# Value loads of the late attention tiles: issued by SyncE instead of ScalarE

## The chip, the cores and the metric

The kernel runs on one core of a Trainium2 chip. The metric is the device time of one execution in microseconds (us). Five engines run their own instruction streams in program order: TensorE (PE, its weight loads PEld), VectorE (DVE), ScalarE (ACT), GpSimd (POOL) and SyncE (SP). SP only issues DMA transfers here; ACT and POOL issue some beside their computing. An engine that issues a DMA first waits for whatever the transfer depends on, and all that stands behind it on that engine waits with it.

## What is computed

A chunked attention with memory slots, and two gated feed-forward layers on its output. All inputs of the attention are float32.

```python
def _attn_ref(q, k, v, mem_k, mem_v):            # q, k, v: (4, 8, 768, 64); mem: (4, 8, 8, 64)
    chunk, left_ctx, right_ctx = (32, 16, 8)
    for c in range(S // chunk):
        q_c = q[:, :, c_start:c_end]
        k_full = concatenate([mem_k, k[:, :, l_start:r_end]], axis=2)
        v_full = concatenate([mem_v, v[:, :, l_start:r_end]], axis=2)
        a = softmax(scale * q_c @ k_full.T)
        out[:, :, c_start:c_end] = a @ v_full

x = attn_out.transpose(0, 2, 1, 3).reshape(3072, 512)
x = sigmoid(x @ w_gate) * (x @ w_val) @ w_out         # moe:  512 -> 1536 -> 512
h = x @ w_in;  out = (h * sigmoid(1.702 * h)) @ w_out # moe2: 512 -> 2048 -> 512
```

## The kernel before

The 3072 tokens are cut in two ways: into 32 attention tiles of 96 queries (three chunks each, eight per batch entry), and into six blocks of 512 columns for the matrix products. Blocks 0 to 3 go through the first feed-forward layer one after the other (`first_product` L821 and L828, `gated`, `gemm2` L1020); blocks 4 and 5, and then the whole second layer, use another scheme of products (L1318, L1655). Each float32 product is done as three passes over a high and a low part, so that PE has work in nearly all of the time.

Attention for blocks 1 to 5 is woven into those products. Nine tiles are done early by a path with PE transposes. The other 23, the **late tiles**, are walked in a fixed order, `nth` = 0 to 22. For one of them:

- SP loads the queries in 12 small transfers and the keys in some 16 to 20 for each pair of tiles (`f<-in_q_dram`, `raw<-in_k_dram`, and `f<-in_mem_k_dram` for each new batch entry). Both have two sets of buffers. DVE turns them (`ev_q` L532, `ev_k` L540), ACT adds the memory keys (`ev_m` L544).
- PE does one **burst**: first the products with the values (`pe_pv`, L704) of an older tile, then the scores of this tile (`pe_s`, L555). From the fourth tile on, the burst of tile n holds the values' products of tile n-2, from a list `late` of tiles not yet finished.
- The softmax follows on DVE, ACT and POOL; then `rest()` of the tile that came before: it loads that tile's values and memory values into `vn`, POOL scales its probabilities, and DVE turns them into `pt` (L670). `evict` takes the burst's result to the next layer's input (L758, L761), or, for blocks 4 and 5, through `qt` (L733) to a scratch tensor by a store that ACT issues (`x_dram<-qt`).

There is one buffer `vn` for all late tiles. The value load of tile n-1 has therefore to wait for the burst of tile n, whose products read the values of tile n-2, and has to land before the burst of tile n+1. A value load is one transfer of up to 120 rows and one of the 8 memory rows; a tile at the start or the end of a batch entry has a third one, for its clamped edge rows. Over the 23 late tiles that makes 28 + 23 = 51 transfers.

The order of all instructions on all engines is written by the class `Schedule`, a planner in the kernel file: tasks have an engine, an estimated length and dependencies; due times are passed back from the products and from the bursts (burst n is due at 150 + 12.6 n us by `PACE`, L388), and at each step the ready task with the earliest due time goes next on its engine. In `dma()` (L345) the issue of a transfer is a task of 0.45 us on "sp", or on "act" where `act=True`; key loads are given 0.62 us. The due time of a task on "sp" is passed back with 2.0 us and its bytes' time added for the landing (`lat`, L66), that of a task on "act" without. So the argument `act` changes the plan as well as the issuing engine.

ACT also issues the stores of the first layer's results (`y_dram<-f`, L1044). In the same stage SP loads, after the last queries, the inputs of the next stage (L1194, L1304, L292).

Of the kernel before, what the change touches and what calls it, by code (L numbers as in the profile page):

```python
# [136 lines left out]
def c_act(n):  # L137
    return 0.13 + n / 1200.0
# [7 lines left out]
def kernel(  # L146
# [198 lines left out]
    def dma(dst, src, key, r=(), act=False, dur=0.45, pool=False):  # L345
        n = 8
        for d in src.shape:
            n *= d
        q_ = nc.gpsimd if pool else nc.scalar if act else nc.sync
        add("pool" if pool else "act" if act else "sp", dur, lambda: q_.dma_start(out=dst(), in_=src), r=list(r), w=[key], nbytes=n)  # L350
# [39 lines left out]
    def attention(t, bufs, banks, pe_path, extra=None, nth=0, last=False):  # L390
# [11 lines left out]
        def tadd(eng, dur, fn, r=(), w=(), more=0.0, **kw):  # L402
            add(eng, dur, fn, r=r, w=w, slack=SL + more, **kw)

        def load_ctx(name, src, mem, act=False):

            s0 = j * TQ - LEFT
            r0 = LEFT if j == 0 else 0
            r1 = TK - RIGHT if j == TPB - 1 else TK
            parts = [(r0, r1, src[b, :, s0 + r0 : s0 + r1, :]), (TK, P, mem[b])]  # L410
            if j == 0:
                parts.append((0, LEFT, src[b, :, 0:LEFT, :]))
            if j == TPB - 1:
                parts.append((r1, TK, src[b, :, S - RIGHT : S, :]))
            ks = []
            for i, (a, z, s) in enumerate(parts):
                ks.append((kk[name], i))
                dma(lambda a=a, z=z: T[name][a:z], s.rearrange("h s d -> s h d"), ks[-1], r=pre, act=act)
            for i in range(len(parts), 4):
                ks.append((kk[name], i))  # L420
            return ks
# [197 lines left out]
        def norm(eng, dst, rows_, keys):  # L619
            r = slice(*rows_)  # L620
            c = slice(*keys)
            n = rows_[1] - rows_[0]
            eng.tensor_tensor(  # L623
                out=dst, in0=e3()[r, :, c], in1=T["sm"][r].to_broadcast([n, H, keys[1] - keys[0]]), op=ALU.mult
            )

        if pe_path:

            def ev_norm(c):
                r = (c * CH, (c + 1) * CH)  # L630
                eng = nc.vector if en[c] == "dve" else nc.gpsimd
                norm(eng, T["pw"][r[0] : r[1], :, c * CH : c * CH + CTX], r, (0, CTX))

            def ev_norm_m():
                norm(nc.vector if en[0] == "dve" else nc.gpsimd, T["pw"][:, :, TK:P], (0, TQ), (CTX, KW))

            en = ["pool", "pool", "pool"] if t in (0, 2) else ["dve", "pool", "pool"]
            for c in range(NCK):
                tadd(en[c], 0.75 if en[c] == "dve" else 1.2, lambda c=c: ev_norm(c), r=ke + [kk["sm"]], w=[(kk["pw"], c)])
            tadd(en[0], 0.25 if en[0] == "dve" else 0.35, ev_norm_m, r=ke + [kk["sm"]], w=[(kk["pw"], 3)])  # L640

            def pe_pt(n):
                for h in range(H):
                    a, p = divmod(h, NP)
                    nc.tensor.transpose(  # L645
                        bt[a][:, p * TQ : p * TQ + n], T["pw"][:n, h, :], ident()[:n, :n]
                    )

            def ev_pt(a, n):
                src = bt[a][:, : NP * TQ].rearrange("p (h s) -> p h s", s=TQ)[:, :, :n]  # L650
                dst = T["pt"].rearrange("p (a h) s -> p a h s", a=2)[:, a, :, :n]
                nc.scalar.activation(dst, src, AF.Copy)

            def probs(n, more=()):
                bands = range(4) if n == TQ else (0, 3)
                r = [(kk["pw"], c) for c in bands] + [bufs.kid, *more]
                tadd("pe", 0.7 if n == TQ else 0.45, lambda: pe_pt(n), r=r, w=kbt, margin=mg)
                for a in range(2):
                    tadd("act", c_act(NP * n), lambda a=a: ev_pt(a, n), r=[kbt[a]], w=[(kk["pt"], a)])
        else:  # L660

            def ev_norm():
                norm(nc.gpsimd, T["pn"][0:L, :, 3 * CH - NM : 3 * CH], (0, L), (CTX, KW))
                norm(nc.gpsimd, T["pn"][L:TQ, :, CTX:KW], (L, TQ), (CTX, KW))

            PTB = ((0, 0, 0), (1, 0, 1), (2, 0, 2), (0, 1, 1), (1, 1, 2), (2, 1, 3), (0, 2, 3), (1, 2, 3))

            def ev_pt(part):
                for c, kb, r in PTB[2 * part : 2 * part + 2]:
                    nc.vector.transpose(  # L670
                        T["pt"][r * CH : (r + 1) * CH, :, c * CH : (c + 1) * CH],
                        T["pn"][c * CH : (c + 1) * CH, :, kb * CH : (kb + 1) * CH],
                    )

            def rest():
                load_ctx("vn", v, mem_v, True)
                tadd(
                    "pool",
                    0.95,
                    lambda: norm(nc.gpsimd, T["pn"][:, :, 0:CTX], (0, TQ), (0, CTX)),  # L680
                    r=ke + [kk["sm"]],
                    w=[(kk["pn"], 0)],
                )
                tadd("pool", 0.6, ev_norm, r=ke + [kk["sm"]], w=[(kk["pn"], 1)])
                for part in range(4):
                    tadd(
                        "dve",
                        0.88,
                        lambda part=part: ev_pt(part),
                        r=[(kk["pn"], 0), (kk["pn"], 1)],  # L690
                        w=[(kk["pt"], part)],
                    )
# [74 lines left out]
        if pe_path and t != NPRO - 1:  # L767
            probs(TQ)
            tadd("pe", 0.8, pe_pv, r=rp, w=[kbv], margin=mg)
            evict()  # L770
        elif pe_path:
            probs(CH)
            tadd("pe", 0.5, lambda: pe_pv(CH), r=rp, w=[kbv])
            evict(0)
            probs(TQ, [kbv])
            tadd("pe", 0.8, lambda: pe_pv(TQ, bq), r=rp, w=[kbq])
            held_back.append(lambda: evict(1, bq, [kbq]))
        else:
            late.append(dict(pv=pe_pv, rp=rp, evict=evict, rest=rest))
            if last:  # L780
                for x in list(late):
                    if x is not late[0]:
                        x["rest"]()
                    tadd("pe", 0.9, x["pv"], r=x["rp"], w=[kb0, kb1])
                    x["evict"]()
                late.clear()
# [1113 lines left out]
```

## Time and profile before

| | |
|---|---|
| time, median of three | 1128.76 us (1127.51 to 1131.07) |
| the profiled execution's own time | 1130.38 us |
| its span | 1128.6 us |
| busy in the span: PE / DVE / ACT / POOL | 1116.4 / 842.4 / 589.6 / 161.6 us |
| share of PE in the chain that ended last | 97% |
| granted TensorE clock | 1.00 in all stages |
| DMA queue of SP (q1) | 201560 packets, 162.29 MB |
| DMA queue of ACT (q10) | 37368 packets, 15.47 MB |

The span counts from the first to the last instruction; 1.8 us of the execution's time lie around it. The late tiles run from about 133 us (first query load on SP) to 460 us. Matmuls are pipelined and their ends modelled, so a busy PE says only that no gap between them was seen.

### The profile page before, as it was taken

Reading aid. Unit: us, or ns where it says so; the run is one execution under the profiler, and the core shown is the slowest. Engines: PE = TensorE matmul, PEld = TensorE weight load, DVE = VectorE, ACT = ScalarE, POOL = GpSimd, SP = SyncE. Lnnn points to the kernel's source line nnn. Section 1 sums busy time; section 2 is a strip of 40 time slices with the busy share of each in tenths; the row PEclk is TensorE's granted clock in tenths of the full one; section 3 lists DMA queues with packets and bytes.
Section 4 is the critical chain, followed back from the end, with each engine's and each line's share of the span. In section 5 each row is a group of like instructions: output and inputs, shape, how many; then the busy total and the mean of one; then the engine's idle time right before and its main releaser. Section 6 shows DMA issues by size and latency. Waiting matters only on the chain.

```text
span 1128.6 us, 19515 instructions
## 1 busy us (share of the span) xinstructions
PE 1116.4 (99%) x7190; PEld 933.7 (83%) x7190; DVE 842.4 (75%) x1440; ACT 589.6 (52%) x972; POOL 161.6 (14%) x209
## 2 busy tenths in 40 slices
PE   7999999999999999999999999999999999999998
PEld 6888899997888888888888888888888888888886
DVE  7989746776767788888887788869966369575365
ACT  5888632222222344676666777666455365354452
POOL 4332244122333113200001110000000000000000
PEclk9999999999999999999999999999999999999999
DMA  9676344335433555542556867868796666776526
GB/s 208 203 216 196 90 122 114 52 67 119 102 83 79 150 145 174 199 161 104 177 178 245 305 216 269 271 244 295 245 255 211 200 203 219 233 216 204 170 86 176
DMA packets 245903, 203.13 MB, mean 180 GB/s; under 512 B 170928, under 2 KB 191920, under 8 KB 245808
## 3 DMA queue, kind: packets, MB, share of 16 engines
q1 hardware_dynamic: 201560, 162.29, 48.9%
q0 software_dynamic: 6880, 24.12, 5.7%
q10 hardware_dynamic: 37368, 15.47, 5.0%
q8 instruction: 57, 0.93, 0.3%
q14 instruction: 38, 0.31, 0.1%
HBM read 151.49 MB, written 50.33 MB: 179 GB/s over the span
## 4 chain that ended last, share of the span: by engine, by line
PE 97%; DMA 1%; SPq 1%; ACT 0%; DVE 0%; issue 0%; ACTq 0%
PE bank L1318 30%; PE bank L1655 20%; PE bank L1020 18%; PE bank L821 15%; PE bank L828 8%; PE both L704 2%; PE both L555 2%; SPq L350 1%; PE bank L704 1%; PE bank L885 0%; DMA kn<-in_mem_k_dram 0%; PE bank L645 0%; DMA vn<-in_v_dram 0%; DMA w<-wo_dram 0%; PE both L645 0%
## 5 line engine op out<-in xcount | busy, mean ns | idle before, releaser
L1318 PE MATMUL bank<-sb_x,sb_r 128*128 128x512 f32 x1512 | 347.4, 389 | 0.0
L1318 PEld LDWEIGHTS bank<-sb_x,sb_r 128*128 128x128 f32 x1512 | 283.8, 188 | 58.9
L1655 PE MATMUL bank<-wq,w 128*128 128x512 f32 x756 | 178.0, 389 | 0.4 <-DMA w<-wo_dram 0.4
L1655 PEld LDWEIGHTS bank<-wq,w 128*128 128x128 f32 x756 | 141.8, 188 | 30.3 <-issue 0.8
L821 PE MATMUL bank<-xh,w 128*128 128x512 f32 (+1 forms) x464 | 159.6, 355 | 0.0
L821 PE MATMUL bank<-xl,w 128*128 128x512 f32 (+1 forms) x464 | 158.6, 353 | 0.0
L1334 DVE TENSOR_TENSOR sb_s<-bank,sb_s 128x512 f32<-128x512 f32 x108 | 74.4, 690 | 83.0 <-PE bank L1318 75.8
L828 PE MATMUL bank<-xh,w 128*128 128x512 f32 (+1 forms) x464 | 108.8, 356 | 0.0
L1020 PE MATMUL bank<-gh,wq 128*128 128x512 f32 (+1 forms) x448 | 98.7, 360 | 0.0
L821 PEld LDWEIGHTS bank<-xh,w 128*128 128x128 f32 x464 | 87.8, 189 | 12.6
L821 PEld LDWEIGHTS bank<-xl,w 128*128 128x128 f32 x464 | 87.8, 189 | 11.9
L1330 ACT ACTIVATE sb_s<-bank 128x512 f32<-128x512 f32 x108 | 64.8, 604 | 50.7 <-PE bank L1318 49.9
L828 PEld LDWEIGHTS bank<-xh,w 128*128 128x128 f32 x464 | 78.1, 189 | 12.4
L1020 PEld LDWEIGHTS bank<-gh,wq 128*128 128x128 f32 x448 | 76.4, 189 | 12.9
L670 DVE STREAM_TRANSPOSE pt<-raw 32x256 f32<-32x256 f32 x184 | 79.5, 432 | 4.7 <-POOL raw L623 2.1
L1626 DVE TENSOR_TENSOR wq<-xh_g,wq 128x1024 fp32r<-128x1024 f32 (+1 forms) x60 | 60.5, 1008 | 22.9 <-ACT wq L1623 22.5
L1623 ACT ACTIVATE wq<-xh_g 128x1024 fp32r<-128x1024 f32 (+1 forms) x60 | 53.3, 889 | 35.2 <-PE bank L1655 34.2
L853 ACT ACTIVATE gh<-sig 128x512 fp32r<-128x512 f32 (+1 forms) x58 | 32.3, 557 | 67.4 <-DVE sig L848 61.6
L623 POOL TENSOR_TENSOR raw<-e,sm 96x448 f32<-96x448 f32 (+2 forms) x69 | 41.0, 606 | 176.1 <-DVE sm L615 149.0
L1655 PE MATMUL bank<-wq,w_e 128*128 128x512 f32 x252 | 62.5, 389 | 0.0
L845 ACT ACTIVATE sig<-bank 128x512 f32<-128x512 f32 (+1 forms) x58 | 30.5, 526 | 55.5 <-PE bank L828 49.7
L1655 PEld LDWEIGHTS bank<-wq,w_e 128*128 128x128 f32 x252 | 47.3, 188 | 9.8
(215 smaller groups left out, 1646.1 us busy)
## 6 DMA issues: line engine op xcount, KB each, us to landing
sb_r<-wc_dram SPq DMA_DIRECT2D x133, 256.0 KB
w<-wo_dram SPq DMA_DIRECT2D x63, 512.0 KB
w_e<-wo_dram SPq DMA_DIRECT2D x21, 512.0 KB
wc_dram<-sb_r SPq DMA_DIRECT2D x15, 512.0 KB
wo_dram<-w POOLq DMA_DIRECT2D x14, 512.0 KB, 3.9
raw<-in_moe_w_out_dram SPq DMA_DIRECT2D x13, 512.0 KB
raw<-in_moe_w_in_dram SPq DMA_DIRECT2D x13, 512.0 KB
wf_dram<-f POOLq DMA_DIRECT2D x24, 256.0 KB, 2.9
```

What stands on the lines that cost most here:

```text
L623: eng.tensor_tensor(out=dst, in0=e3()[r, :, c], in1=T["sm"][r].to_broadcast([n, H, keys[1] - keys[0]]), op=ALU.mult)
L670: nc.vector.transpose(T["pt"][r * CH : (r + 1) * CH, :, c * CH : (c + 1) * CH], T["pn"][c * CH : (c + 1) * CH, :, kb * CH : (kb + 1) * CH],)
L704: nc.tensor.matmul((bk if to is None else to)[hp * D : (hp + 1) * D, o : o + q], T["vn"][:, 2 * p + hp, :], T["pt"][:, hp * NP + p, :q], s ...
L821: nc.tensor.matmul(bank[bk][:, :n], w[:, 0, ts[t]], x[xb][:, t, c0 : c0 + n], start=t == 0 and x is xhs, stop=False)
L828: nc.tensor.matmul(bank[bk][:, :n], w[:, 1, ts[t]], xhs[xb][:, t, c0 : c0 + n], start=False, stop=t == NK - 1)
L1020: nc.tensor.matmul(bank[into[m]][:, c0 : c0 + n], w[:, wi, m * P : (m + 1) * P], g[:, :n], start=f == 0 and j == 0 and c0 == 0, stop=f == ...
L1318: nc.tensor.matmul(bank[bk], w[:, o : o + P], xt[x, k][:, xl, :], start=first and k == 0 and wl == 0 and xl == 0, stop=k == 1 and wl == 1, ...
L1330: add("act", c_act(BLK), lambda: nc.scalar.activation(work[n], bank[bk], AF.Copy), r=[("bank", bk)], w=[n])
L1334: nc.vector.tensor_tensor(out=work[n], in0=bank[bk], in1=work[n], op=ALU.add)
L1623: nc.scalar.activation(quad[b_][:, c, 0, :], src(js), AF.Copy)
L1626: nc.vector.tensor_tensor(out=quad[b_][:, c, 1, :], in0=src(js), in1=quad[b_][:, c, 0, :].bitcast(F32), op=ALU.subtract)
L1655: nc.tensor.matmul(bank[bk], lhs, quad[b_][:, x, gl_, :], start=begin, stop=last and x == js[-1] and wl == 1, skip_group_check=not first,)
```

## The change

`rest()` of a late tile calls `load_ctx` for the values without its last argument, `act`, so that it takes its default, `False`. The 51 transfers are issued by SP, and are tasks of "sp" in the plan. ACT keeps the stores (`y_dram`, `x_dram`, and a few of the output).

```diff
@@ -673,7 +673,7 @@
             def rest():
-                load_ctx("vn", v, mem_v, True)
+                load_ctx("vn", v, mem_v)
                 tadd(
                     "pool",
                     0.95,
```

## Rows read from the trace of the kernel before

**Rows 1.** Busy time by stage: bounds in us, length, then each engine's busy time

```profile
core 0: us, PE busy (x) PEld busy (x) DVE busy (x) ACT busy (x) POOL busy (x), PEclk, DMA share, GB/s
0.00:20.00 20.00, 14.00 (x296) 12.09 (x301) 13.67 (x24) 10.58 (x22) 7.84 (x14) 1.00 0.95 183
...
120.00:240.00 120.00, 120.00 (x1292) 112.97 (x1291) 81.53 (x168) 39.46 (x85) 37.33 (x50) 1.00 0.39 90
...
280.00:320.00 40.00, 39.14 (x342) 31.42 (x341) 29.13 (x60) 10.46 (x20) 12.12 (x17) 1.00 0.44 96
320.00:480.00 160.00, 160.00 (x1295) 129.84 (x1294) 127.02 (x257) 64.03 (x112) 43.41 (x61) 1.00 0.52 141
...
720.00:900.00 180.00, 179.62 (x793) 148.41 (x792) 126.14 (x170) 95.78 (x142) 0.00 (x0) 1.00 0.76 249
900.00:1128.60 228.60, 223.84 (x991) 184.86 (x989) 145.12 (x179) 107.09 (x154) 0.57 (x2) 1.00 0.63 189
```

**Rows 2.** Waits of PE: us in total, times, longest us

```profile
PE bank L1020 <- ACT f L1040: 0.9, 1, 0.9
...
PE bank L1655 <- DMA w<-wo_dram: 0.4, 1, 0.4
```

**Rows 3.** Timeline of ACT, 274 to 284: start, us, instruction, [idle before]

```profile
275.60 0.46 ACTq L350 DMA_DIRECT2D vn<-in_v_dram  x1
277.10 0.31 ACTq L350 DMA_DIRECT2D vn<-in_mem_v_dram  x1
277.45 0.28 ACT L544 ACTIVATE kt<-f 128x96 f32<-128x96 f32 x1 [2.43 <-DMA y_dram<-f]
280.13 0.28 ACTq L350 DMA_DIRECT2D vn<-in_v_dram  x1
280.46 0.63 ACT L853 ACTIVATE gh<-sig 128x512 fp32r<-128x512 f32 x1 [2.72 <-DMA vn<-in_v_dram]
```

**Rows 4.** Timeline of PE at 282

```profile
282.11 0.50 PE L1020 MATMUL bank<-gh,w 128*128 128x512 f32 x1 [0.86 <-ACT f L1040]
```

**Rows 5.** Chain that ended last, 258 to 300: start, us, what

```profile
275.60 4.50 DMA vn<-in_v_dram
```

**Rows 6.** Timeline of ACT, 246 to 254: another tile with three transfers

```profile
248.86 0.28 ACTq L350 DMA_DIRECT2D vn<-in_mem_v_dram  x1
251.79 0.28 ACTq L350 DMA_DIRECT2D vn<-in_v_dram  x1
```

**Rows 7.** DMA issues of line L350, 133.9 to 262.4: count, min/median/max ns

```profile
L350 SPq DMA_DIRECT2D f<-in_q_dram x120: 311/430/1766, 133.9 to 262.1; - x120
L350 SPq DMA_DIRECT2D raw<-in_k_dram x108: 311/439/1912, 134.8 to 253.9; - x108
...
L350 SPq DMA_DIRECT2D f<-in_mem_k_dram x12: 279/298/1313, 143.6 to 256.4; - x12
...
L350 ACTq DMA_DIRECT2D vn<-in_v_dram x9: 279/332/635, 142.5 to 258.8; - x9
L350 ACTq DMA_DIRECT2D vn<-in_mem_v_dram x8: 278/290/466, 145.2 to 260.5; - x8
...
DMA to landing us min/median/max: 2.3/2.5/3.7
```

**Rows 8.** Timeline of SP, 256 to 274: issues of one kind merged

```profile
256.81 11.29 SPq L350 DMA_DIRECT2D f<-in_q_dram  x24
```

**Rows 9.** Timelines of DVE and PE: queries of one late tile, then its scores

```profile
265.59 0.56 DVE L532 STREAM_TRANSPOSE qt<-f 128x384 f32<-128x384 f32 x1
...
273.27 0.74 PE L555 MATMUL both<-kt,qt 64*32 64x64 f32 x48
```

**Rows 10.** Waits of SP's queue, 134 to 262: us in total, times, longest us

```profile
SPq L350 <- DMA vn<-in_v_dram: 2.4, 2, 1.2
```

**Rows 11.** The stage's end: timelines of SP (410 to 470) and PE (440 to 442)

```profile
435.30 0.82 SPq L1194 DMA_DIRECT2D xh_y<-x_dram  x2
...
440.80 0.88 PE L704 MATMUL both<-pt,vn 128*64 128x96 f32 x16
```

## The prediction

> **What bounds the kernel now.** I read the busy time by stage first [rows 1]. PE is busy for 120.00 of 120 us from 120 to 240, for 160.00 of 160 from 320 to 480, and so on; its clock is at the upper of its two levels (1.00) in every stage. Since "busy" is modelled for PE, the second view is the waits of PE [rows 2], which should show whatever the first one hides: between 20 us and the last stage there are two waits that count, 0.9 us in the late tiles and 0.4 us long after them. The sum of the gaps is 6.00 us in the first 20 us, 0.86 us from 280 to 320, 0.38 us from 720 to 900, and 4.76 us in the last stage [rows 1]. The change can touch neither the start nor the end: the late tiles lie between 133 and 460 us. So the kernel is bound by the number of its matmuls, and **all that a better late stage can give back is 0.86 us**, or 1.24 us if the new order happens to mend the later gap as well.
>
> The third view is the place of that 0.86 us gap. PE waits until 282.11 for ACT's copy L1040 [rows 4]. On ACT [rows 3] a value load was issued at 275.60, the memory rows at 277.10, the memory keys' copy at 277.45; then nothing until 280.13, when the third value load of this tile is issued, and only after it the copies that PE needs. The chain that ended last runs through just that [rows 5]: the first value load, 4.50 us long, lands at 280.10, and the third is issued 0.03 us later. So ACT stood still because a transfer that it had to issue waited for an earlier one to land. I take it that the two share a completion counter; the rows show the wait, not its reason. Five of the 23 late tiles have a third load. In another one ACT stands from 248.86 + 0.28 to 251.79 for the same reason [rows 6], and PE has no gap there.
>
> **The change, part by part.**
>
> *Taken from ACT.* 51 issues (28 + 23) at a median of about 0.33 and 0.29 us [rows 7], 51 x 0.31 = 16 us of issuing, and the waits that go with them. ACT is computing for 64.03 of the 160 us from 320 to 480 [rows 1], so the issue time itself is worth nothing. Of the waits one reaches PE: **-0.86 us**, between 0 (another wait ends as late) and -0.86. What is next late behind it is the gate's copy L853 at 280.46, which had its input before: it waited 2.72 us for the value load alone [rows 3]. I take the whole 0.86.
>
> *Added to SP.* This is where the cost can lie. In the first half of the late tiles SP issues without a pause: 120 + 108 + 12 = 240 transfers from 133.9 to 262.4 us [rows 7], 128.5 / 240 = 0.54 us each with all waits, and 11.29 / 24 = 0.47 us each in an undisturbed stretch [rows 8]. SP is thus as full as PE is, and its fullness is covered only by how far it is ahead. I measure that at the tenth late tile. Its 12 query loads are the first half of the 24 that begin at 256.81, so the last is out at 256.81 + 11.29 / 2 = 262.5. DVE turns the queries at 265.59, and PE uses them at 273.27 [rows 9]. DVE could have begun at 273.27 - 0.56 = 272.7, which leaves 7.1 us. To that comes what lies between landing and 265.59: of the 3.1 us since the last issue a landing takes some 2.3, going by the shortest that the profile gives (for POOL's transfers, [rows 7]), so that 0.8 us are left. The cover is 7.9 us.
>
> Up to there ACT issued 9 + 8 = 17 value transfers [rows 7]. By the planner's due times each tile's values go in front of the queries that are due for the same burst, so all 17 would stand before these queries on SP: 17 x 0.47 = 8.0 us. That is as much as the cover, so **I take 0 us** for the issue alone, with nothing in hand. For later tiles the cover grows: the queries are limited there by their two buffers and no longer by SP.
>
> *Waits added to SP.* The value load of a tile waits for a burst on PE, and behind it on SP now stand the keys and queries of the next tiles. SP may also wait for the value load's landing a few issues later; it already does so twice in this stretch, 2.4 us in all, 1.2 at the longest [rows 10], while ACT is the issuer. The lower bound of the added waits is 0: the plan puts the load where the burst is due, and a queue that is late itself never waits. It can't be below 0. The upper bound is one such wait of 1.2 us for each of the 8 tiles before, 9.6 us. The value nearer to the rows is the lower: 2 waits for 8 tiles, and these are there already. I take 0 and keep 9.6 for the range.
>
> What the Trainium skill says speaks against the change here: by "DMA: Bandwidth & Descriptors", section "Anatomy of one DMA", the DMA engines themselves never wait on a semaphore; the wait is spent on the issuing sequencer before dispatch. The trace agrees, by ACT's 2.72 us in front of L853 [rows 3]. By that rule each wait that leaves ACT turns up on SP; the same page, section "Issuing engines are not separate DMA queues", has it that the choice of issuer saves issue time alone. By the first rule the time would be that of the first rival below; by the second one it would not move.
>
> *The values themselves.* They are due a burst later, some 12 us after they may be issued; 4.50 us is the landing on the critical chain [rows 5]. SP would have to be over 7 us behind with them before PE noticed. At the end of the stage SP sits in waits of its own: it issues the next stage's first loads only at 435.30, and the burst at 440.80 needs values [rows 11]. Were they put behind these loads, they would go out at 436.1 and land, with 4.50 us, at 440.6: just in time. **0 us**, at most a few tenths.
>
> *The new plan.* SP's and ACT's tasks are planned anew, and with them the order on DVE and PE from 133 us on. The trace of before can't show that order. Its price is bounded by gaps of the size that the stage has, 0.86 us each: from -0.86 (the one gap, which is in the sum already) to some four new ones, +3.4. I take 0, since PE has none in 120 to 240 and none in 320 to 480, through some twenty bursts.
>
> The sum is **-0.86 us**: 1130.38 - 0.86 = 1129.5 for an execution like the profiled one. That one lay 1.6 us over the median of 1128.76, so the median goes to **1127.9 us**.
>
> **The rivals.**
>
> *SP becomes the pace of the late tiles (slower).* At the tenth tile PE stands in front of its scores until the queries are there. Price: 8.0 us of issues and up to 9.6 us of waits against 7.9 us of cover, so a shortfall of 0.1 to 9.7 us; with half of the waits it is 4.9 us. It decides from the point where SP's extra time by 262 us passes 7.9 us. For it: SP has no pause in that stretch. Against it: the planner counts SP's tasks too, and puts the bursts later in PE's order if it sees SP late; PE then does products first. Time: 1127.9 + 4.9 = 1132.8, up to 1137.6.
>
> *ACT is held all the same (no change).* The stores stay on ACT, and it waited for transfers that it hadn't issued itself, as for the store in front of 277.45 [rows 3]. Then the gap stays, or moves to another tile: 1128.8.
>
> *The new order opens small gaps.* One to four of them, 0.86 us each: 1128.8 to 1131.3.
>
> **How the numbers follow.** About 0.3%, 3.4 us, is what a measurement of this kernel can tell from no change. The forecast has a chance of 0.34, ACT held all the same 0.12, small gaps 0.18 (a third of that beyond 3.4 us over the median), SP as the pace 0.32 (six tenths of it beyond, where the shortfall is over 4.3 of its 0.1 to 9.7 us), and 0.04 is left for a gain over 3.4 us, for which no row shows a source. Slower by over 0.3%: 0.06 + 0.19 = 0.25. Faster: 0.04. Within: 0.71. The range begins at 1126.5, the lowest time of before (1127.51) with the 0.86 us taken off and rounded down; it ends at 1136.5, which takes in most of the first rival and leaves out its upper end, with the faster case about 1 in 10.
>
> **What would show it.** In the trace of the changed kernel: no value load on ACT's queue; PE's wait for L1040 at about 282 us gone; SP's issues from 133 us on without a pause for longer than before, and the tenth tile's queries out some 8 us later, at about 270. If SP paces, PE's waits have new rows at L555 or L704, and DVE's turn L532 starts right after the last query load lands. I am wrong if PE is busy for less than 119 of the 120 us from 120 to 240, if its gaps lie outside the late tiles, or if ACT still stands for 3 us at a transfer.

## The result, and the profile after

The changed kernel takes 1136.12 us (median of six, 1134.58 to 1138.62) against 1128.74 us (1127.51 to 1131.07): ratio 1.0066, 95% interval 1.0051 to 1.0082. It is **7.4 us slower**, where the forecast was 0.9 us faster. The time lies just inside the forecast's range (1126.5 to 1136.5), at the end that the first rival had set. The profiled execution took 1138.62 us, with a span of 1136.8 us against 1128.6; it was the longest of the six, so its gaps may be larger than most.

The busy time by stage answers to [rows 1] (columns as there; the last two rows are stretches inside the stage above them):

```profile
core 0: us, PE busy (x) PEld busy (x) DVE busy (x) ACT busy (x) POOL busy (x), PEclk, DMA share, GB/s
120.00:240.00 120.00, 120.00 (x1295) 113.12 (x1294) 82.78 (x169) 38.76 (x84) 35.95 (x50) 1.00 0.39 88
280.00:320.00 40.00, 40.00 (x347) 32.47 (x346) 28.78 (x57) 9.67 (x18) 12.54 (x17) 1.00 0.45 99
320.00:480.00 160.00, 153.47 (x1247) 124.01 (x1246) 118.76 (x241) 57.18 (x98) 39.71 (x59) 0.97 0.51 132
403.40:410.20 6.80, 5.83 (x72) 4.79 (x73) 3.13 (x6) 1.71 (x4) 0.00 (x0) 0.50 0.34 55
458.00:461.40 3.40, 3.40 (x9) 2.64 (x10) 3.28 (x8) 2.57 (x4) 0.06 (x1) 0.50 0.83 195
```

From 120 to 240 us PE is as full as before, and the gap of 0.86 us between 280 and 320 is gone. All the loss is behind 320 us: 6.53 us without work, and 10.2 us in which the granted clock is at the lower of its two levels (0.50, 1.2 GHz). The waits of PE say what it stood for, in place of [rows 2] (us in total, times, longest):

```profile
PE both L704 <- DMA vn<-in_mem_v_dram: 4.1, 1, 4.1
PE both L704 <- DVE w L1422: 2.4, 1, 2.4
```

Both are at L704, the products with the values. PE's timeline at the first of them (start, us, instruction, idle before):

```profile
389.38 0.88 PE L704 MATMUL both<-pt,vn 128*64 128x96 f32 x16
...
399.84 0.39 PE L821 MATMUL bank<-xl,w 128*128 128x512 f32 x1
404.37 1.55 PE L704 MATMUL both<-pt,vn 128*64 128x96 f32 x16 [4.14 <-DMA vn<-in_mem_v_dram]
405.85 1.09 PE L555 MATMUL both<-kt,qt 64*32 64x64 f32 x48
406.88 2.07 PE L828 MATMUL bank<-xh,w 128*128 128x512 f32 x4
...
411.28 1.08 PE L828 MATMUL bank<-xh,w 128*128 128x512 f32 x4
```

The burst of values at 389.38 ended at 390.26 and made the buffer `vn` free for the values of tile n=17. The next burst could have begun at 400.2; it began at 404.37. And the four products L828 right behind it take 2.07 us, where the same four take 1.08 us at 411.28: the gap is paid a second time, in part, by the clock. Where the values were is told by SP's timeline (issues of one kind merged):

```profile
384.73 0.81 SPq L350 DMA_DIRECT2D raw<-in_k_dram  x2
387.20 12.73 SPq L350 DMA_DIRECT2D f<-in_q_dram  x24
399.97 0.92 SPq L350 DMA_DIRECT2D raw<-in_k_dram  x2
400.99 0.91 SPq L350 DMA_DIRECT2D vn<-in_v_dram  x2
401.94 0.33 SPq L350 DMA_DIRECT2D vn<-in_mem_v_dram  x1
```

They stood behind 24 query and two key loads, and went out at 400.99, 10.7 us after they could have. I call this time the **lag**: the start of a tile's value load, less the end of the burst that freed the buffer. For n = 1 to 22, worked out from the timelines of SP (ACT before) and PE, in us:

```
before  0.7 1.9 0.8 1.0 0.8 0.8 0.8 2.3 0.8 0.8 0.8 0.8 0.8 0.8 2.0 0.7  1.2 3.4 0.8 1.5 0.8 0.1
after   0.0 0.0 0.4 1.6 2.4 2.6 3.6 5.4 8.3 6.2 6.4 6.2 6.6 5.8 7.3 7.6 10.7 4.7 2.9 0.0 0.0 0.0
```

It grows over 16 tiles without a wait on PE, and then it is too long: at n=17 the bursts stand 10.8 us apart (389.38 to 400.2), most others 12.6. Less the burst (0.88) and the landing (2.3 us for one load at this place, 3.3 for the three from the first issue on), that leaves 6.6 to 7.6 us.

SP itself no longer waits for free buffers, so its lead is used up. Waits of SP's queue from 140 to 400 us, first before, then after:

```profile
SPq L350 <- DVE qt L532: 5.1, 3, 3.2
SPq L350 <- DMA vn<-in_v_dram: 3.9, 4, 1.2
...
SPq L350 <- DVE kt L540: 2.1, 2, 1.4
```

```profile
SPq L350 <- DMA y_dram<-f: 8.2, 5, 3.3
SPq L350 <- DMA x_dram<-qt: 0.8, 1, 0.8
SPq L350 <- DMA f<-in_q_dram: 0.5, 1, 0.5
```

Before, 7.2 us of waits are for DVE to free a buffer of queries or keys: SP was ahead. After, none is. SP's waits for landings are the same in sum, 9.9 us before and 10.0 after (all rows of the two views), but most of them, 8.2 us, are now for `y_dram` stores that ACT issued, on whose data the loads don't depend.

The second stall, 2.39 us at 457.04 with 3.4 us of low clock, belongs to n=21: its values were issued at 446.54 with no lag and landed at 456.79, 10.25 us later. PE could have gone on at 454.65, 8.1 us after the issue. The row names DVE's L1422, whose work ended at 456.87; but in the trace the counter (semaphore) of this value load is the one that holds PE until 456.8. So the second stall is a slow landing and not a late SP. From the last burst of values (457.13 before, 465.11 after) everything is late by 8 us, and so is the end.

### The profile page after: what moved, and what is told of

Its sections match the earlier page's. It is cut to its first block, busy times and chain, and to the rows that moved or that the text cites. A ratio compares the mean times of both kernels' runs of the same rounds, so it can differ in the third digit from the quotient of the medians.

```text
span 1136.8 us, 19523 instructions
## 1 busy us (share of the span) xinstructions
PE 1122.9 (99%) x7190; PEld 939.3 (83%) x7190; DVE 843.9 (74%) x1440; ACT 588.6 (52%) x972; POOL 158.9 (14%) x209
## 4 chain that ended last, share of the span: by engine, by line
PE 95%; DMA 2%; DVE 1%; SPq 1%; ACT 0%; issue 0%; DVEq 0%; ACTq 0%
PE bank L1318 30%; PE bank L1655 20%; PE bank L1020 17%; PE bank L821 15%; PE bank L828 8%; PE both L704 2%; PE both L555 2%; DMA f<-in_q_dram 1%; SPq L350 1%; PE bank L885 1%; PE bank L704 0%; PE bank L645 0%; DVE pt L670 0%; DMA qn<-in_q_dram 0%; PE bank L444 0%
## 5 line engine op out<-in xcount | busy, mean ns | idle before, releaser
L828 PE MATMUL bank<-xh,w 128*128 128x512 f32 (+1 forms) x464 | 110.4, 360 | 0.0
L828 PEld LDWEIGHTS bank<-xh,w 128*128 128x128 f32 x464 | 79.0, 191 | 12.6 <-issue 0.2
L848 DVE SCALAR_TENSOR_TENSOR sig<-sig,bank 128x512 f32<-128x512 f32 (+1 forms) x58 | 34.0, 586 | 30.1 <-PE bank L828 29.4
```

The source lines that it names most:

```text
L828: nc.tensor.matmul(bank[bk][:, :n], w[:, 1, ts[t]], xhs[xb][:, t, c0 : c0 + n], start=False, stop=t == NK - 1)
L848: nc.vector.scalar_tensor_tensor(out=sig[:, :n], in0=sig[:, :n], scalar=1.0, in1=bank[src_val][:, :n], op0=ALU.add, op1=ALU.mult)
```

## The experiments

Lags are worked out as above. "Before" in each comparison is the kernel before on the same chip; its median differs by up to 1.5 us from chip to chip, so compare ratios, not times.

**Plan or queue?** The argument `act` changes both. The first run keeps the plan of before, and with it the order on PE, DVE and POOL, and changes the issuer alone; the second has the plan of after and leaves the issuing to ACT.

```diff
-        q_ = nc.gpsimd if pool else nc.scalar if act else nc.sync
+        q_ = by or (nc.gpsimd if pool else nc.scalar if act else nc.sync)
...
-                dma(..., r=pre, act=act)
+                dma(..., r=pre, act=act, by=nc.sync if act else None)
```

```diff
-                load_ctx("vn", v, mem_v, True)
+                load_ctx("vn", v, mem_v, by=nc.scalar)
```

> The value loads are issued by SP, but stay tasks of ACT in the plan, so that the orders on PE, DVE and POOL are those of the kernel before. Theory Q (SP's queue is late, and the values stand behind queries and keys in it): the loss comes with the queue alone, 1133 to 1140 us, PE has waits at L704 or L555 between 250 and 460 us, and the lag from a burst to its value load grows along the stage as it does in the changed kernel (from 0 to 10 us). Theory P (the new plan, with another order on PE and DVE, is what costs): within 1 us of 1128.7.

> The plan of the changed kernel, word for word on PE, DVE and POOL, but the value loads are issued by ACT. Theory Q: the two waits of PE at L704 (4.1 and 2.4 us) and the low clock behind them are gone, 1127.5 to 1130 us. Theory P: 1134 to 1138 us, as the changed kernel.

Issuer alone: 1149.14 us, ratio 1.0159 (1.0136 to 1.0181). Plan alone: 1130.42 us, ratio 1.000 (0.999 to 1.001). So the new plan in itself costs nothing, the queue costs 18 us, and the plan that counts the transfers on SP gives back some 11 of them. PE's waits with the issuer alone changed:

```profile
PE both L704 <- DMA vn<-in_v_dram: 4.6, 2, 3.5
PE both L704 <- DMA vn<-in_mem_v_dram: 3.6, 3, 2.7
PE bank L821 <- DVE xl L761: 3.5, 1, 3.5
PE bank L821 <- DVE sig L848: 2.5, 2, 2.0
```

**Is it the values, or the place that they take?** Before, with 51 dummy transfers on SP at the places of the run above; the real values stay on ACT.

```diff
+                tw = (pad0[a:z, :192]..., s[:3]...) if act else None
...
             q_.dma_start(out=dst(), in_=src)
+            if twin_:
+                nc.sync.dma_start(out=twin_[0], in_=twin_[1])
```

> The plan of the kernel before, values on ACT as there; beside each of the 51 value transfers SP issues a transfer of three of the eight heads into an unused buffer, at the place in SP's order where e1 has the value transfer. Nothing reads it and it waits for no burst. Theory Q1 (SP's issue time alone makes the queries late, and PE waits for these): about the loss of e1, 1140 to 1150 us, with waits of PE at L555. Theory Q2 (queries have room enough; what costs is that the values themselves stand in the late queue, and the waits for bursts in front of them): within 3 us of the kernel before, no wait of PE at L704 over 1 us.

1149.28 us, ratio 1.0159 (1.0136 to 1.0183): as much as with the real values on SP. The real values are on time here: their lag is 0.7 to 3.7 us but for one tile (7.3 at n=16). PE's waits, then two of DVE's (line numbers are 7 higher):

```profile
PE bank L828 <- DVE xl L768: 5.8, 1, 5.8
PE bank L828 <- DVE sig L855: 4.8, 2, 4.1
PE bank L1027 <- ACT f L1047: 1.3, 1, 1.3
```

```profile
DVE xl_y L301 <- DMA xl_y<-in_moe_w_in_dram: 9.0, 1, 9.0
DVE f L519 <- DMA f<-in_mem_k_dram: 7.3, 1, 7.3
```

No wait for the values is left (at L704, here L711, PE waits 0.3 us in all). Other loads of SP come late: the memory keys, begun at 261.09 against 254.39 before, and a weight of the next stage, at 388.09 against 370.75. DVE stands at their turn, in its fixed order, and what PE waits for at 266.0 and 396.7 is the work behind that turn. The dummies also move bytes of their own, but the issuer alone moved none more than before and cost the same. So SP's time is the cost, whatever it is spent on, and which of its loads comes too late depends on the order.

**Where is the lag built up?** After, with the values on ACT up to tile 16; with the memory rows alone on ACT; and with tiles 21 and 22 alone on ACT. (The second diff is against before.)

```diff
-                load_ctx("vn", v, mem_v)
+                load_ctx("vn", v, mem_v, nth < 17)
...
-                dma(..., r=pre, act=act)
+                dma(..., r=pre, act=act and i == 1)
...
-                load_ctx("vn", v, mem_v)
+                load_ctx("vn", v, mem_v, nth >= 21)
```

> Values on SP only for the last six late tiles (nth 17 to 22), on ACT for the others. If SP's lag is built up by the issues of the tiles before, the value load of tile 17 now goes out within 5 us of its burst and PE's wait of 4 us for it is gone: 1129 to 1132 us. If its place behind 24 query loads in SP's order is enough by itself: the wait stays, 1133 to 1136 us.

> Only the 28 transfers of values go to SP; the 23 transfers of memory rows stay on ACT, in the plan too. Theory Q with the issue time as its cause: SP's extra work is about half, the lag of the value loads at 400 us falls from 10 to some 5 or 6 us, and PE has no wait of 4 us there: 1128 to 1132 us. If the lag comes from SP's waits for ACT's stores instead (8.2 us in five waits from 133 to 400 us), it stays near 9 to 10 us and so does the time, 1134 to 1137.

> The changed kernel with the values of the last two late tiles (nth 21 and 22) on ACT again. The second wait of PE (2.4 us at 457 us, with the value load of 446.54 landing only after 10.25 us) is in question. If the load is late because it is in SP's queue: that wait goes, the first (4.1 us at 404) stays, and the time falls by about 3 us, to 1132 to 1134 us. If it is late because POOL's 512 KB transfers of the same moment go ahead of it on the DMA engines whoever issues it: the wait stays and so does the time, 1135 to 1137 us.

Values on SP from tile 17 on only: 1130.18 us, ratio 1.000 (0.9991 to 1.001), lag at n=17 3.6 us. The very load that stops PE in after does no harm when the tiles before it left SP its time. Memory rows on ACT: 1138.37 us, ratio 1.007 (1.0045 to 1.0094), a miss: the lag at n=17 is 9.1 us, for SP now waits 9.5 us, in nine places, for the landing of those rows, which ACT issued. Tiles 21 and 22 on ACT: 1136.98 us, ratio 1.006 (1.0041 to 1.008). The second stall is gone, and in its place PE waits 1.7 us at L555 for the queries' turn; the first stall stays (4.4 us), and nothing is won where some 3 us were expected. In two of the runs below, which leave that load on SP (`y_dram` stores on POOL, both stores on POOL), it landed after 7.7 and 8.0 us, in time for the burst, and the second stall is gone there too.

**Issues or waits for stores?** Five kernels on why SP is late. The first leaves the memory rows out of after where the batch entry is still the same (they are in the buffer already), and so plans without them; the second does the same in place, with the plan and all orders as in after; the third has the stores of `y_dram` issued by POOL, the fourth those of `x_dram` too; the last joins the second and the fourth. (In the diff: `continue` is the first, `skip` the second, then the two stores.)

```diff
-                load_ctx("vn", v, mem_v)
+                load_ctx("vn", v, mem_v, False, fresh)
...
+                if i == 1 and not rows:
+                    continue
...
+        add(..., lambda: skip or q_.dma_start(out=dst(), in_=src), ...)
...
-                nc.scalar.dma_start(out=y_dram[...], in_=st[:, :n])
+                nc.gpsimd.dma_start(out=y_dram[...], in_=st[:, :n])
...
                         act=True,
+                        by=nc.gpsimd,
```

> The changed kernel without the loads of memory rows that are in the buffer already: they are loaded only where the batch entry changes, so that SP has some 18 issues fewer and nothing goes back to ACT. If the lag is SP's issue time, 17 tiles with one transfer less (0.5 us each) cut it at tile 17 from 10.7 to some 3 to 6 us, PE's wait of 4 us goes: 1129 to 1132 us. If the lag comes from waits, it stays: 1134 to 1137 us.

> After's plan and order, untouched; the memory rows of a value load are simply not issued where the batch entry hasn't changed (some 18 of the 23; the rows are still in the one buffer). So the places on SP that the run with the same rows left out of the plan had given to other loads stay empty here: ahead of the values of n=17 stand some 14 transfers fewer, 490 in place of 504. Theory (the values are late because of the number of transfers that stand ahead of them in SP's order, at 0.5 us each): their lag at n=17 falls from 10.7 us by some 7 us to 3 to 5 us, PE's wait of 4.1 us at L704 is gone, time 1128.5 to 1131.5, unlike the run with a new plan (1139.6). Rival (SP is held by waits for buffers and for stores, and takes what it is given): lag 9 to 11 us, L704 waits 3 us and more, time 1135 to 1140.

> The changed kernel with the 24 y_dram stores of L1044 issued by POOL instead of ACT, the plan and SP's order as in the changed kernel. If SP's waits for these stores (8.2 us in five waits) carry the lag: they are gone, the value load of the burst at 404 us goes out before 395, PE's wait of 4.1 us there vanishes with its low clock, 1129 to 1132 us. If the issue time of the 51 loads alone carries it: the wait stays at 3 us or more, 1134 to 1137 us.

> After, with the stores of both kinds (the first layer's results and the values' results for blocks 4 and 5) issued by POOL instead of ACT; plan and SP's order as in after. In after SP waited 8.2 us for the first kind and 0.8 us for the second before 400 us. Theory (these waits are what SP lacks): lag of the values of n=17 falls from 10.7 to 3 us or less, no wait over 1 us at L704, time 1128.5 to 1131.5. Rival (the issues alone fill SP; a wait taken away is only replaced by the next): lag 8 to 11 us, L704 waits 3 us or more at about 404 us, 1133 to 1137.

> The run with the memory rows left out in place (14 transfers fewer ahead of the values of n=17, order as in after), and both kinds of stores on POOL besides. There SP had lost 1.5 us of its gain to one wait of 2.6 us for a store at 379.5. If issues and waits for stores together make the lag: 14 x 0.5 = 7 us of issues plus the waits are gone, lag at n=17 at most 3 us, no wait at L704, time 1128.5 to 1131. If SP is held by the freeing of its buffers: lag 8 to 11 us as before, 1133 to 1137.

| kernel | time, us | ratio (95%) | lag at n=9, n=17, us |
|---|---|---|---|
| after | 1136.12 | 1.0066 (1.0051 to 1.0082) | 8.3, 10.7 |
| rows not planned | 1139.57 | 1.0076 (1.0057 to 1.0096) | 8.6, 10.0 |
| rows left out in place | 1135.64 | 1.0053 (1.0040 to 1.0067) | 7.1, 10.9 |
| `y_dram` stores on POOL | 1135.2 | 1.0042 (1.0026 to 1.0058) | 7.8, 10.9 |
| both stores on POOL | 1132.92 | 1.0034 (1.0017 to 1.0051) | 6.0, 10.2 |
| rows in place and both stores | 1129.27 | 1.0005 (0.9995 to 1.0015) | 3.7, 2.9 |

Neither half is enough; both together bring back the time of before, with all values still on SP. (The profiled execution with both stores on POOL was the longest of its six, 1137.76 us, so its lag may stand at the upper end.)

That fewer transfers alone don't help has two reasons. In the first kernel the planner filled the free places: counted in SP's order of the plan, 500 transfers stand ahead of the values of n=17, against 504 in after. In the second 490 do, but what SP won it lost again to stores. Its waits from 140 to 400 us:

```profile
SPq L350 <- DMA y_dram<-f: 6.1, 5, 2.0
SPq L350 <- DMA x_dram<-qt: 4.0, 2, 2.6
SPq L350 <- PE both L704: 1.3, 2, 0.9
```

It needs 226 us from the values of n=1 to those of n=17, as after does, for 413 transfers in place of 427. Its SP timeline ahead of n=17, and then that of the kernel with both changes:

```profile
385.71 14.62 SPq L350 DMA_DIRECT2D f<-in_q_dram  x24
400.37 0.92 SPq L350 DMA_DIRECT2D raw<-in_k_dram  x2
401.39 0.91 SPq L350 DMA_DIRECT2D vn<-in_v_dram  x2
```

```profile
391.67 0.92 SPq L350 DMA_DIRECT2D raw<-in_k_dram  x2
392.69 1.15 SPq L350 DMA_DIRECT2D vn<-in_v_dram  x2
393.88 0.33 SPq L350 DMA_DIRECT2D vn<-in_mem_v_dram  x1
```

With both changes the same 413 transfers take 218 us, and the same load goes out 8.7 us earlier. PE's waits there are small:

```profile
PE both L704 <- issue: 1.6, 1, 1.6
PE both L704 <- DMA vn<-in_mem_v_dram: 0.9, 1, 0.9
PE both L555 <- DVE qt L532: 0.2, 1, 0.2
```

**Is it the planner's estimate?** In the plan of after SP has no pause before 400 us and no value load is more than 3.1 us behind; real SP took 0.529 us a transfer between n=1 and n=17 where the plan has 0.507, which over 427 transfers is 9.4 us. Two kernels tell the planner 0.03 us more for each SP transfer of the late tiles: after, and after with the rows not planned.

```diff
+        dur += 0.03 if sp_more[0] and not act else 0.0
```

> After with one number of the planner changed: each SP transfer of the late tiles is estimated 0.03 us longer (0.48 and 0.65 in place of 0.45 and 0.62), about what SP really took between the second and the eighteenth value load (0.529 us a transfer against 0.507 in the plan). The transfers are the same 51, all on SP; but the planner now puts 490 ahead of the values of n=17 in place of 504, and the bursts later in PE's order, behind more products. Theory (SP runs some 10 us behind its plan, and PE's order rests on the plan): lag at most 6 us, no wait at L704 over 1 us, time 1128.5 to 1131.5. Rival (SP can't carry the 51 transfers in this stage, whatever the order): the waits stay or move to L555 or to the products, 1133 to 1140.

> The two together with a new plan: memory rows loaded only for a new batch entry (some 18 transfers fewer), and the planner told 0.03 us more for each SP transfer. Theory: the plan's order is kept, lag at most 5 us, no wait at L704 over 1 us; 1128 to 1130.5, that is, before's time within 0.2%. Rival (fewer transfers don't help, as in the run with the rows left out alone): 1133 to 1140.

1139.94 us, ratio 1.0090 (1.0076 to 1.0104), and 1135.21 us, ratio 1.0049 (1.0036 to 1.0063). A miss: the values' waits are down to 1.2 us by name, but the bursts come later and PE stands in many small places instead, as in the first of the two:

```profile
PE both L707 <- issue: 3.0, 1, 3.0
PE bank L1023 <- ACT gh L856: 2.0, 1, 2.0
PE both L707 <- ACT e L583: 1.6, 1, 1.6
PE both L707 <- DMA f<-in_q_dram: 1.5, 1, 1.5
```

A plan that knows SP's pace doesn't make SP faster.

**What is the one gap worth?** After, plan and order untouched, with the three transfers of tile 17 issued by ACT; then those of 17 and 21.

```diff
-                load_ctx("vn", v, mem_v)
+                load_ctx("vn", v, mem_v, by=nc.scalar if nth == 17 else None)
...
+                load_ctx("vn", v, mem_v, by=nc.scalar if nth in (17, 21) else None)
```

> After, plan and order untouched; the three value transfers of n=17 alone are issued by ACT, at the place that they have in the common order. Theory (the gap at 404 us is this one load behind 24 query loads): the 4.1 us wait is gone, and with it the 6.8 us at the lower clock, which cost some 3.4 us; 1136.1 - 7.5 = 1128.6, to 1131 if a part comes back at the next burst. Rival (the whole of SP's work is late, and the next burst or the queries stop PE instead): 1133 to 1137, with a new wait of 2 us or more between 404 and 425.

> As the run before, and the values of n=21 on ACT too. Both places of the two long waits of after are then free of SP: no wait over 1 us at L704, 1128 to 1130. If the waits move on (as with tiles 21 and 22 given back, where a wait of 1.7 us for the queries' turn took their place): 1131 to 1134.

1137.55 us, ratio 1.0071 (1.0053 to 1.0089), and 1137.04 us, ratio 1.0065 (1.0048 to 1.0082): nothing is won. The gap at 404 us is gone and the lag of n=17 is 0.8 us, but that of n=18 is now 9.9 and 10.5 us (4.7 in after). The stalls move on by a burst; in the second kernel:

```profile
417.26 0.88 PE L704 MATMUL both<-pt,vn 128*64 128x96 f32 x16 [2.78 <-DMA vn<-in_mem_v_dram]
425.53 0.50 PE L821 MATMUL bank<-xh,w 128*128 128x512 f32 x1 [1.06 <-DVE sig L848]
```

In after the stall of n=17 had given SP 4.1 us, and the slow stretch behind it, to catch up. Without it the lateness is still there, and the next load shows it. The gaps of PE add up to 7.0 and 8.7 us, more than in after (6.5), but the granted clock stays at 1.00.

**Something faster than both?** Before, with the memory rows loaded only for a new batch entry.

```diff
-                load_ctx("vn", v, mem_v, True)
+                load_ctx("vn", v, mem_v, True, fresh)
```

> Before, values on ACT, with the memory rows loaded only for a new batch entry: some 18 issues fewer on ACT. Can it beat before? All that the late stage can give back is the one gap of 0.9 us, which comes from the third value transfer and not from the memory rows: 1128.0 to 1129.5, ratio 0.999 to 1.001. If ACT's issue time (18 x 0.3 = 5 us) did hold PE somewhere: 1126 or less.

1129.66 us, ratio 0.9998 (0.9989 to 1.0007): no change within the interval. The trace shows no wait of PE from 130 to 480 us, not even the 0.86 us of before, so PE has nothing left in this stage that could be given back.

## Why the prediction was wrong

**"-0.86 us" from ACT: right.** PE is full from 280 to 320 us, and the third value load no longer stands ahead of ACT's copies [rows 3, 4].

**"Added to SP ... I take 0 us": the step that failed.** At the tenth tile itself the zero was right. The sum had the cover of 7.9 us used up, with the queries out at about 270; they were out at 266.9, 4.4 us later than before, and DVE takes them as they land, while PE uses them at 272.38 [rows 8, 9], so that 3.1 us of the cover are left:

```profile
268.70 0.58 DVE L532 STREAM_TRANSPOSE qt<-f 128x384 f32<-128x384 f32 x1 [0.33 <-DMA f<-in_q_dram]
```

The error is the next sentence: "for later tiles the cover grows". I had worked out one place, 17 transfers into 51, found nothing in hand there, and let the rest of the stage be free. SP has no pause to speak of until 400 us, and every further tile puts two or three more transfers on it. The 7.2 us that SP waited for buffers before are the slack that the rows show from 140 to 400; the 21 + 17 value transfers ahead of n=17, of about 0.45 us, are 17 us. By this estimate SP is 9.9 us short there; the lag is 10.7. That sum was to be had from the views I had read.

**"SP would have to be over 7 us behind": right as a bound, wrong as a reason for 0.** The room at n=17 is 6.6 to 7.6 us; SP was 10.7 us behind. The last tiles, where I looked for the danger [rows 11], had no lag; the second stall came there all the same, by a landing of 10 us in place of 4.50 [rows 5].

**"Waits added to SP": 0 taken, right in sum, but not for the reason given.** The waits I bounded, for the values' burst on PE, are not there, and the waits for landings are as long as before. But "a queue that is late itself never waits" is wrong: SP is late and still waits 9.0 us for ACT's stores, of a kind that I had read from [rows 10] for the value loads alone. When SP is ahead such a wait can be hidden in the one for its buffers; when it is late it counts in full. With both kinds of stores on POOL about half of the loss is left (ratio 1.0034 against 1.0066).

**Why it waits for them** can be read from the counters (semaphores) that the trace names for each transfer. From 130 to 410 us the transfers of SP and ACT take turns on the same eight (101 to 105, 107, 108, 110), those of POOL on eight others (111 to 118), and SP, as the program has it, issues a transfer only when the one before it on the same counter has landed. The longest wait in after, 3.35 us, is a query load issued at 271.55 on counter 101, which ACT's store issued at 267.91 held until 271.53. In the kernel before, the first and the third value load of [rows 3] both have 104: the prediction's guess was right.

**"The new plan: 0": right** for the plan by itself (ratio 1.000), but not for what it is worth against a full queue, some 11 us.

**The first rival was what happened.** "SP becomes the pace", 1132.8 up to 1137.6, has the cause of the first stall, the sign and the size. Three things differ. It was to stand at the queries and at the tenth tile; it stands at the values, at n=17. The second stall is not its doing, for SP was not late there. And its price is not the shortfall alone: the gaps come to 6.5 us, and 9.2 us of work at the lower clock cost, by estimate, half of that, 4.6 (some 4 us of both belong to the second stall). That makes 11.1 us. The bursts say 10.0: the values of n=14 are done 2.0 us earlier than before (363.3 against 365.3), the last ones 8.0 later; 1.1 us I can't place. "ACT is held all the same" and "small gaps" didn't come about. And none of the three signs by which I would be wrong showed: PE is full from 120 to 240 us, its new gaps lie in the late tiles, and ACT's longest wait for a transfer there is 2.4 us. The first was set for the stretch that I had worked out, and the loss came behind it; the other two could not tell the forecast from the first rival.

**What the pages said.** The text weighed two rules of the Trainium skill, "DMA: Bandwidth & Descriptors". The one in "Issuing engines are not separate DMA queues" says that issuing from several engines saves only the time on the sequencer, which is usually small relative to the DMA itself. For one transfer that agrees with the trace, 0.43 us of issue against 2.3 us and more to the landing; on a full queue 51 of them are worth 18 us. And it isn't all that the issuer decides here: moving ACT's stores to POOL takes no issue off SP, and about half of the loss goes with their waits.

**What stays open.** In the profiled execution with both stores on POOL the time freed of waits came back as longer issues (0.472 us each against 0.458, from n=1 to n=17), and I can't say why. That POOL's transfers make the landing at n=21 slow is argued from their nearness alone.

## What to carry to other kernels

Before moving issues to a queue, sum the queue over the whole stage, not up to one tile: its slack is the time that it waits for free buffers, and when the added issues are longer than that, the lag grows from tile to tile until some load is late. Order is then only a choice of which load; giving back the one that stops the engine moves the stall to the next. A queue's waits for transfers of another engine, with which it shares counters, count as issue time as soon as the queue is late.

## What the runs showed of the hardware that I had not expected

- With the gap of 4.14 us on PE went 6.8 us at the lower clock (403.4 to 410.2, 5.8 of them with work), with that of 2.39 us 3.4 us (458.0 to 461.4, when PE was at work again). Four products L828 took 2.07 us in place of 1.08. The length of a gap alone doesn't tell: one of 1.90 us (rows not planned) was followed by 3.4 us at the lower clock, while gaps of 2.98 us (planner told) and 2.78 us (values of 17 and 21 on ACT) cost no clock, nor did the 0.86 us of before [rows 1].
- SP has an issue of over 1.1 us, up to 2.0, most of them some 10 to 15 us apart (18 between 133 and 404 us in after, 15 before). The 22 and 24 issues over 0.6 us in that stretch take 18.7 and 19.8 us more than the usual 0.43 each. In after they help to lift the mean issue to 0.46 us; the rest of the 0.53 us that a transfer costs lies between the issues.
- A value load took 10.25 us to land when POOL had issued three transfers just ahead of it (at 444.84, 445.43 and 446.13), and 7.7 and 8.0 us in the two runs with stores on POOL, behind the same three; the five between 400 and 434 us in after took 2.6 to 3.4 us. Three transfers of POOL aren't all of it: in before, behind those at 440.0, 440.6 and 442.4, the load at 442.45 took 5.4 us.
